# A fused attention and FFN kernel: Mish with fewer VectorE operations, and a new written-out order for the first FFN

## The chip, the cores and the metric

The kernel runs on one core of a Trainium2 chip. The time is the device time of one execution in microseconds. Engines are TensorE (PE), VectorE (DVE), ScalarE (ACT), GpSimd (POOL) and SyncE (SP), which here issues the transfers.

## What is computed

```python
x = attention(q, k, v)            # 2 x 8 heads, 768 x 64; keys 0..7 and the last 96, slope bias
h = x @ w_in                      # 1536 x 512 @ 512 x 2048, float64 weights
sp = where(h > 20, h, log1p(exp(min(h, 20))))
x = (h * tanh(sp)) @ w_out        # Mish, back to 1536 x 512
p = probs / (probs.sum(-1) + 1e-9)
out = sum(p[:, e] * (relu(x @ w1[e]) @ w2[e]) for e in range(4))   # 512 -> 1024 -> 512
```

## The kernel before

The 1536 tokens are worked on in three blocks of 512. For the first block, attention (16 pairs of heads and 128-row tiles) and then the first FFN run by themselves; behind them comes a loop over steps in which the experts of block 0, then the FFN of blocks 1 and 2 go on, with the attention of blocks 1 and 2 woven into the first 31 steps. A last stage does the experts of blocks 1 and 2.

**The first FFN** has 16 steps, one for each 128 columns of `w_in`. A step s consists of these pieces, each with a letter in the string `PLAN`, which `first_block` executes letter by letter and which so fixes the order on every engine:

- narrowing chunk s of the weights from float64: `a` is ScalarE's Abs (L602), each `t` is one of three VectorE operations (L605, L607, L609). The float64 chunk is a 1 MB load into one of four buffers (`big`, `raw`; the list `TURN` says which); a finished chunk is also stored to DRAM (L613, 0.5 MB), and the next load into the buffer is issued when the third `t` is through.
- `H`: the hidden group on TensorE (L783, four f32 matmuls of 512 columns).
- Mish of the 128x512 tile h. With E = exp(h) and n = E(E+2), it is h n/(n+2), where r = 1/(n+2) is made by ScalarE as exp(-ln(n+2)) and then refined by a Newton step: `e` ScalarE Exp (L663), `c` cap (L670), `n` (L677), `l` ScalarE's Ln and Exp (L682, L683), then u (L687), m (L692), v (L698) and the gate g (L702), all on VectorE but `e` and `l`.
- `P`: the project group (L795, four matmuls into four accumulator banks).

`w` letters split the first expert chunks into two fp32r parts (L629 on ScalarE, L632 on VectorE). At the string's end `i` issues the loads of the next attention pairs (SP), `j` splits their queries and keys into parts (L234, L236 on ScalarE, L239, L241 on GpSimd for the first two pairs and on VectorE after that), and `1` to `6` are the parts of one attention round: load ahead, scores s (L260, L261), softmax (L274, L285), normalization and splits of further pairs (L190 to L195, L249, L250), transposes pt (L200, L297, L298), and o (L307, L315). A round's transposes and o belong to the one and two rounds before it, so a round started alone has neither.

**The loop** (`run`) does in step s the hidden group H of twelve fp32r matmuls (L647), one attention round and the project group P of step s - 1 (L748). Step 16 is its first. At steps 23, 31 and 39 (`EXTRA = 7, 15, 23`) a second, extra round is done around the hidden group. The FFN steps in it use the same Mish functions, with `e` in PSUM.

Of the kernel before, what the change touches and what calls it, by code (L numbers as in the profile page):

```python
# [15 lines left out]
P = 128  # L16
# [8 lines left out]
NF1 = 16  # L25
# [18 lines left out]
    "CSEZAEADVVFTXTCEZAAaDVVTtTCaAZtAFtHtttteHcatntlHteaumcvnegcPtlatumtHvngtlPteuamvcHgntltaPeucmtvgHntl"  # L44
    "tauPetmvgcPntltauHtmvgtePcntlatHutmteHvcagntltPeumavgHcntltuPetmcvnHgtlutPmevgcntlPumvgHtttePtcnlHau"
    "mtvtaHgetictnPetlcutHmwvgnwlPweuwcmvgHnwlwuwmPevcgnwlwPumvgjj1P23456"
# [4 lines left out]
    "l": ["n"], "u": ["l"], "m": ["u"], "v": ["m"], "g": ["v"], "P": ["g"],  # L51
# [3 lines left out]
TURN = [0, 1, 2, 3, 0, 1, 2, 3, 0, 1, 2, 3, 0, 1, 0, 1]  # L55
FREE = {2: 4, 3: 8}
EXTRA = 7, 15, 23
# [100 lines left out]
class Pair:  # L158
# [173 lines left out]
class FirstPair(NarrowPair):  # L332
# [206 lines left out]
class Body:  # L539
# [138 lines left out]

    def mish_r(self, s):

        nc, (e, n, r) = self.nc, self.enr[s]
        nc.scalar.activation(r, n, AF.Ln, bias=2.0)  # L682
        nc.scalar.activation(r, r, AF.Exp, scale=-1.0)  # L683

    def mish_u(self, s):
        nc, (e, n, r) = self.nc, self.enr[s]
        nc.vector.scalar_tensor_tensor(e, n, 2.0, r, ALU.add, ALU.mult)  # L687

    def mish_m(self, s):
        nc, (e, n, r) = self.nc, self.enr[s]  # L690
        self.nr[s] = self.temp("nr", s, bufs=1)
        nc.vector.tensor_tensor(self.nr[s], n, r, ALU.mult)  # L692

    def mish_v(self, s):
        nc, (e, n, r) = self.nc, self.enr[s]
        nr = self.nr.pop(s)
        self.enr[s] = e, n, nr if e is r else r
        nc.vector.scalar_tensor_tensor(self.enr[s][2], e, 2.0, nr, ALU.subtract, ALU.mult, reverse0=True)  # L698
# [321 lines left out]
    def first_block(self, ready, now):  # L1020
# [5 lines left out]
        n = dict.fromkeys("SXEDNTCAFHecnlumvgPatw", 0)  # L1026
# [77 lines left out]
        def begin_next(k):  # L1104
            assert n["t"] >= 36
            then.load(4)
# [7 lines left out]
            "u": self.mish_u, "m": self.mish_m, "v": self.mish_v, "g": self.gate_first, "P": project,  # L1114
# [12 lines left out]
        return then, n["P"]  # L1127


    def run(self):  # L1130
# [39 lines left out]
        for s in range(s0, last):  # L1170
# [143 lines left out]
```

## Time and profile before

| | us |
|---|---|
| median of 3 runs (lowest to highest) | 902.6 (899.82 to 902.76) |
| the profiled execution | 900.72 |
| its span | 898.8 |

| engine | busy us | share of the span |
|---|---|---|
| PE, matmuls | 875.3 | 97% |
| PE, weight loads | 669.8 | 75% |
| DVE | 622.9 | 69% |
| ACT | 453.5 | 50% |
| POOL | 380.4 | 42% |

The share is a mean over stages with different limits. Matmuls are pipelined, so an interval in which PE counts as busy may still hold some lost time; it is found by comparing when the same kind of group starts. The four stages are the first attention (up to 37 us), the first FFN (to 154), the loop (to 549) and the last stage. A row of a timeline gives start, duration, engine, line, operation, tiles written <- read, shape and count, and in brackets the engine's idle time before it and what ended it.

### The profile page before, as it was taken

What the parts mean: (1) busy time and instruction counts of PE and PEld (TensorE: products, weight loads), DVE (VectorE), ACT (ScalarE), POOL (GpSimd) and SP (SyncE); (2) the same over time, 40 slices, a digit from 0 to 9 for tenths busy, and PEclk for the clock granted to TensorE, in tenths of its full rate; (3) what the DMA queues carried; (4) which work ended last, traced back from release to release, by engine and by line L of the source; (5) the groups of instructions that cost most, each with busy time, mean ns of one, the idle gap of its engine ahead of it and who ended that gap; (6) DMA issues with size and microseconds to landing.
All of it is one profiled execution on the core that took longest, in us unless ns stands there. A gap on an engine that the chain in (4) does not pass through costs nothing.

```text
span 898.8 us, 11323 instructions
## 1 busy us (share of the span) xinstructions
PE 875.3 (97%) x3848; PEld 669.8 (75%) x3848; DVE 622.9 (69%) x1208; ACT 453.5 (50%) x895; POOL 380.4 (42%) x416
## 2 busy tenths in 40 slices
PE   9899999999999999999999999899999999999997
PEld 5534444788888888888888887688888888888886
DVE  6999988867778686588878887435555455554555
ACT  7653335778777776556554456443333333333330
POOL 4000002487868776544401114455544455555420
PEclk9999999999999999999999999999999999999999
DMA  9487361554344442778655650521111111211002
GB/s 325 186 316 261 131 231 50 188 185 167 141 152 153 174 154 72 275 268 299 247 198 187 234 187 1 164 71 47 48 48 47 47 47 47 59 59 47 1 2 97
DMA packets 39859, 126.16 MB, mean 140 GB/s; under 512 B 4080, under 2 KB 6896, under 8 KB 37744
## 3 DMA queue, kind: packets, MB, share of 16 engines
q1 hardware_dynamic: 39648, 125.32, 39.3%
q8 instruction: 32, 0.52, 0.2%
q14 instruction: 35, 0.29, 0.1%
q10 hardware_dynamic: 144, 0.02, 0.0%
HBM read 97.02 MB, written 28.31 MB: 139 GB/s over the span
## 4 chain that ended last, share of the span: by engine, by line
PE 84%; DVE 7%; ACT 3%; DMA 2%; issue 1%; POOL 1%; SPq 0%; DVEq 0%; ACTq 0%; POOLq 0%
PE acc_l L949 20%; PE h L647 18%; PE acc L748 18%; PE ha L904 9%; PE hx L904 7%; PE acc L795 3%; PE h L783 3%; PE pt L200 2%; PE o L307 2%; ACT p L285 1%; DMA big<-in_wff 1%; DVE r L698 1%; DMA w<-in_wts 1%; DMA qk<-in_qk 1%; PE s L261 1%
## 5 line engine op out<-in xcount | busy, mean ns | idle before, releaser
L808 DVE SCALAR_TENSOR_TENSOR big<-acc_l,prob,big 128x512 f32<-128x512 f32 x120 | 88.7, 746 | 77.8 <-PE acc_l L949 77.7
L632 POOL TENSOR_TENSOR wl<-w,wh 128x512 fp32r<-128x512 f32 x90 | 114.8, 1296 | 65.6 <-ACT wh L629 61.7
L887 POOL TENSOR_TENSOR zl<-wout,zh 128x512 fp32r<-128x512 f32 x32 | 40.9, 1300 | 82.5 <-ACT zh L885 82.5
L887 POOL TENSOR_TENSOR sumsl<-bias,sumsh 128x512 fp32r<-128x512 f32 x32 | 41.0, 1302 | 73.4 <-ACT sumsh L885 73.4
L911 ACT COPY raw<-ha 128x512 f32<-128x512 f32 x33 | 19.3, 586 | 81.7 <-PE ha L904 81.7
L783 PE MATMUL h<-x,w 128*128 128x512 f32 x128 | 57.0, 593 | 0.7 <-ACT x L407 0.7
L195 POOL TENSOR_SCALAR p<-p,st 128x256 f32<-128x256 f32 (+1 forms) x58 | 41.5, 727 | 37.8 <-ACT v L249 33.7
L239 POOL TENSOR_TENSOR qs<-raw,qs 64x256 fp32r<-64x256 f32 x2 | 1.9, 967 | 123.3 <-ACT qs L234 123.2
L748 PE MATMUL acc<-wh,gh 128*128 128x512 f32 x128 | 52.5, 410 | 0.0
L629 ACT CAST wh<-w 128x1024 fp32r<-128x1024 f32 x48 | 50.2, 1047 | 1.8 <-DMA w<-in_wts 1.1
L949 PE MATMUL acc_l<-zh,gh 128*128 128x512 f32 x128 | 50.7, 396 | 0.0
L285 ACT ACTIVATE p<-t,st 128x256 f32<-128x256 f32 (+1 forms) x96 | 46.3, 484 | 8.5 <-DVE st L274 8.2
L647 PE MATMUL h<-y0h,wh 128*128 128x512 f32 x128 | 50.4, 394 | 0.0
L949 PE MATMUL acc_l<-zh,gl 128*128 128x512 f32 x128 | 50.5, 394 | 0.0
L949 PE MATMUL acc_l<-zl,gh 128*128 128x512 f32 x128 | 50.3, 393 | 0.0
L949 PE MATMUL acc_l<-zh,gl_late 128*128 128x512 f32 (+1 forms) x128 | 50.3, 393 | 0.0
L949 PE MATMUL acc_l<-zh,gh_late 128*128 128x512 f32 (+1 forms) x128 | 50.3, 393 | 0.0
L647 PE MATMUL h<-y0l,wh 128*128 128x512 f32 x128 | 50.2, 392 | 0.0
L647 PE MATMUL h<-y0h,wl 128*128 128x512 f32 x128 | 50.2, 392 | 0.0
L748 PE MATMUL acc<-wh,gl 128*128 128x512 f32 x128 | 50.2, 392 | 0.0
L748 PE MATMUL acc<-wl,gh 128*128 128x512 f32 x128 | 50.0, 390 | 0.0
L949 PE MATMUL acc_l<-zl,gh_late 128*128 128x512 f32 (+1 forms) x128 | 49.9, 390 | 0.0
(240 smaller groups left out, 2514.6 us busy)
## 6 DMA issues: line engine op xcount, KB each, us to landing
w<-in_wts SPq DMA_DIRECT2D x32, 512.0 KB, 4.5
raw<-in_qkv SPq DMA_DIRECT2D x32, 512.0 KB, 3.6
big<-in_wff SPq DMA_DIRECT2D x10, 1024.0 KB, 6.8
wfirst<-w SPq DMA_DIRECT2D x16, 512.0 KB, 3.0
w<-wfirst SPq DMA_DIRECT2D x16, 512.0 KB, 4.2
wkeep<-wh SPq DMA_DIRECT2D x16, 512.0 KB, 3.0
wkeep<-wl SPq DMA_DIRECT2D x16, 512.0 KB, 2.9
wh<-wkeep SPq DMA_DIRECT2D x16, 512.0 KB, 3.2
```

The costliest lines, as they stand in the source:

```text
L195: engine.tensor_scalar(self.p[:, j, 0:self.nk * P], self.p[:, j, 0:self.nk * P], st[:, 2 + j:3 + j], 0.0, ALU.mult, ALU.add)
L285: nc.scalar.activation(p[:, j, 0:n], t[:, j, 0:n], AF.Exp, bias=self.least[:, j:j + 1], scale=-1.0, accum_out=self.sum[:, j:j + 1])
L629: (nc.vector.tensor_copy if copy == "vector" else nc.scalar.copy)(hi, w)
L632: getattr(nc, engine or "gpsimd").tensor_tensor(lo[:, c], w[:, c], hi.bitcast(F32)[:, c], ALU.subtract)
L647: nc.tensor.matmul(ps, a[:, c], r[:, kc, :], start=m == 0, stop=m == 3 * KC - 1)
L748: nc.tensor.matmul(acc[:, h], a, r, start=opens and k == 0 and m == 0, stop=closes and k == len(chunks) - 1 and m == 2)
L783: self.nc.tensor.matmul(ps, self.w32[s][:, kc * P:(kc + 1) * P], self.x0[:, kc, :], start=kc == 0, stop=kc == KC - 1)
L795: self.nc.tensor.matmul(acc, w[:, 512 + d * P:512 + (d + 1) * P], g, start=s == 0, stop=s == NF1 - 1)
L808: nc.vector.scalar_tensor_tensor(o, acc, p, o, ALU.mult, ALU.add)
L887: nc.gpsimd.tensor_tensor(lo[:, c], w[:, c], hi.bitcast(F32)[:, c], ALU.subtract)
L904: nc.tensor.matmul(ps, a[:, c], r[:, kc, :], start=opens and n == 0, stop=n == 5, skip_group_check=True)
L949: nc.tensor.matmul(o, a[:, c], r[:, w], start=n == 0, stop=n == 5)
```

## The change

Mish: attention's normalization now multiplies its divisor by 0.5, so x and h are twice as large as before, and Exp has scale 0.5. With n = E + 1 (capped), e = n squared, made by ScalarE's Square, and r = 1/(e + 1), the Newton step gives -r, and the gate is (0.5 - r) times 2h. VectorE does cap, u, v and gate; n and m are gone. This holds for all 48 FFN steps. ScalarE's program keeps the one table load that it had. The number of TensorE's program rows stays at 7076.

Order: `PLAN` is written anew; `TURN` runs 0 to 3 throughout; the last two project groups are merged bank by bank (`Q`, `last`); three rounds of the next attention (letters `1` to `6`, three times) stand at the end of `PLAN` instead of one; only step 31 has an extra round (`EXTRA = 15,`); in step 17 the project group of step 16 is issued directly after that step's scores (`follow`).

```diff
 PLAN = (
-    ...
+    ...
 )
-TURN = [0, 1, 2, 3, 0, 1, 2, 3, 0, 1, 2, 3, 0, 1, 0, 1]
+TURN = [0, 1, 2, 3] * (NF1 // 4)
-EXTRA = 7, 15, 23
+EXTRA = 15,
-        nc.vector.tensor_scalar(r, r, 1e-9, None, ALU.add)
+        nc.vector.tensor_scalar(r, r, 1e-9, 0.5, ALU.add, ALU.mult)
...
     def mish_exp(self, s):
-        nc.scalar.activation(e, self.h[s], AF.Exp)
+        nc.scalar.activation(e, self.h[s], AF.Exp, scale=0.5)
     def mish_cap(self, s):
+        e, n = self.enr[s]
+        self.nc.vector.tensor_scalar(n, e, E20, 1.0, ALU.min, ALU.add)
     def mish_n(self, s):
+        e, n = self.enr[s]
+        self.nc.scalar.activation(e, n, AF.Square)
     def mish_r(self, s):
+        nc.scalar.activation(n, e, AF.Ln, bias=1.0)
+        nc.scalar.activation(n, n, AF.Exp, scale=-1.0)
     def mish_u(self, s):
+        nc.vector.scalar_tensor_tensor(self.nr[s], e, 1.0, n, ALU.add, ALU.mult)
-    def mish_m(self, s):
-        nc.vector.tensor_tensor(self.nr[s], n, r, ALU.mult)
     def mish_v(self, s):
+        nc.vector.scalar_tensor_tensor(self.nr[s], self.nr[s], 2.0, n, ALU.subtract, ALU.mult)
     def mish_g(self, s, out=None):
-        nc.vector.tensor_tensor(e if out is None else out, r, self.h.pop(s), ALU.mult)
+        nc.vector.scalar_tensor_tensor(e if out is None else out, self.nr.pop(s), 0.5, self.h.pop(s), ALU.add, ALU.mult)
...
-    def project_first(self, s):
+    def project_first(self, *steps):
...
         for d, acc, _ in self.acc:
+            for k, s in enumerate(steps):
+                self.nc.tensor.matmul(acc, w[k][:, 512 + d * P:512 + (d + 1) * P], g[k], start=s == 0, stop=s == NF1 - 1)
...
+        def last(k):
+            self.project_first(NF1 - 2, NF1 - 1)
...
         def begin_next(k):
-            assert n["t"] >= 36
+            assert n["t"] == 3 * NF1
             then.load(4)
...
+            follow = bool(s0) and s == NF1 + 1
+            if follow:
+                self.project(done)
+                done += 1
             if att and not extra:
                 att.trans()
...
-            if done <= s - (1 if s0 and att and s < need[0] - 2 else 2):
+            if not follow and done <= s - (1 if s0 and att and s < need[0] - 2 else 2):
                 self.project(done)
```

What this does to the engines' programs is shown at three places. Names carry the step's number (h3, gh0, w12) or the block's tile and pair (s4_0); gates are called gh and gl in turn. L783 and L795 are L770 and L783 after the change, L682 and L683 are L676 and L677, and L671 is the Square.

At the start of the first FFN, on TensorE, before:

```order
L783 MATMUL h0_603<-x0_173,w0_405 128x512 x4
L783 MATMUL h1_618<-x0_173,w1_488 128x512 x4
L783 MATMUL h2_633<-x0_173,w2_565 128x512 x4
L795 MATMUL acc0_0_658<-gh0_655,w0_405 128x512
L795 MATMUL acc0_1_659<-gh0_655,w0_405 128x512
L795 MATMUL acc0_2_660<-gh0_655,w0_405 128x512
L795 MATMUL acc0_3_661<-gh0_655,w0_405 128x512
L783 MATMUL h3_678<-x0_173,w3_586 128x512 x4
```

and after:

```order
L770 MATMUL h0_603<-x0_173,w0_405 128x512 x4
L770 MATMUL h1_614<-x0_173,w1_488 128x512 x4
L770 MATMUL h2_633<-x0_173,w2_565 128x512 x4
L770 MATMUL h3_650<-x0_173,w3_586 128x512 x4
L783 MATMUL acc0_0_669<-gh0_648,w0_405 128x512
L783 MATMUL acc0_1_670<-gh0_648,w0_405 128x512
L783 MATMUL acc0_2_671<-gh0_648,w0_405 128x512
L783 MATMUL acc0_3_672<-gh0_648,w0_405 128x512
```

The fourth hidden group now stands ahead of the first project group.

In the middle of the first FFN, on ScalarE, around step 6, before:

```order
L663 ACTIVATE e6_802<-h6_789 128x512
L682 ACTIVATE r6_803<-n6_804 128x512
L683 ACTIVATE r6_803<-r6_803 128x512
L602 ACTIVATE w11_816<-raw1_123 128x1024
L663 ACTIVATE e7_831<-h7_820 128x512
L602 ACTIVATE w12_843<-big0_124 128x1024
```

and after:

```order
L602 ACTIVATE w11_782<-raw1_123 128x1024
L663 ACTIVATE e6_803<-h6_787 128x512
L602 ACTIVATE w12_807<-big0_124 128x1024
L671 ACTIVATE e6_803<-n6_804 128x512
L676 ACTIVATE n6_804<-e6_803 128x512
L677 ACTIVATE n6_804<-n6_804 128x512
L602 ACTIVATE w13_828<-big1_125 128x1024
```

The narrowings of chunks 11 and 12 have moved ahead of step 6's Square, Ln and Exp.

At the end of the first FFN, TensorE up to the loop's first hidden group, before:

```order
L795 MATMUL acc0_3_661<-gh14_1073,w14_966 128x512
L795 MATMUL acc0_0_658<-gl15_1088,w15_974 128x512
L795 MATMUL acc0_1_659<-gl15_1088,w15_974 128x512
L795 MATMUL acc0_2_660<-gl15_1088,w15_974 128x512
L795 MATMUL acc0_3_661<-gl15_1088,w15_974 128x512
L260 MATMUL s4_0_1118<-kh4_0_1092,qs4_0_1090 128x256
L261 MATMUL s4_0_1118<-kl4_0_1095,qs4_0_1090 128x256
L260 MATMUL s4_0_1118<-kh4_0_1092,qs4_0_1090 128x256
L261 MATMUL s4_0_1118<-kl4_0_1095,qs4_0_1090 128x256
L647 MATMUL h16_1145<-y0h_1108,wh16_1018 128x512
```

TensorE there after the change:

```order
L783 MATMUL acc0_3_672<-gl13_1025,w13_828 128x512
L307 MATMUL o4_0_1166<-pt4_0_1082,v4_0_1045 128x256 x4
L783 MATMUL acc0_0_669<-gh14_1075,w14_853 128x512
L783 MATMUL acc0_0_669<-gl15_1136,w15_871 128x512
L783 MATMUL acc0_1_670<-gh14_1075,w14_853 128x512
L783 MATMUL acc0_1_670<-gl15_1136,w15_871 128x512
L783 MATMUL acc0_2_671<-gh14_1075,w14_853 128x512
L783 MATMUL acc0_2_671<-gl15_1136,w15_871 128x512
L783 MATMUL acc0_3_672<-gh14_1075,w14_853 128x512
L783 MATMUL acc0_3_672<-gl15_1136,w15_871 128x512
L647 MATMUL h16_1192<-y0h_1181,wh16_913 128x512
```

and VectorE from the gate of step 14 to the cap of step 15 after the change:

```order
L690 SCALAR_TENSOR_TENSOR gh14_1075<-nr14_1072,h14_1017 128x512
L298 TENSOR_TENSOR pt4_0_1082<-pt4_0_1077,pt4_0_1082 128x4x128
L190 TENSOR_SCALAR st4_1_1067<-st4_1_1067 128x2
L191 RECIPROCAL st4_1_1067<-st4_1_1067 128x2
L195 TENSOR_SCALAR p4_1_1065<-p4_1_1065,st4_1_1067 128x256 x2
L239 TENSOR_TENSOR qs4_3_1097<-raw1_123,qs4_3_1097 64x256
L241 TENSOR_TENSOR kl4_3_1102<-raw1_123,kh4_3_1099 128x512
L632 TENSOR_TENSOR wl18_1091<-w18_708,wh18_1090 128x512 x2
L667 TENSOR_SCALAR n15_1120<-e15_1119 128x512
```

The last two project groups alternate by bank, scores, transposes and o of the first three rounds are ahead of them, and the VectorE work of these rounds stands between the last gates.

## Rows read from the trace of the kernel before

**Rows 1.** Stretches: length, busy us (instructions) of each engine, clock, DMA share, GB/s.

```profile
37.38:75.17 37.79, 34.84 (x80) 15.04 (x80) 35.43 (x50) 16.12 (x22) 0.00 (x0) 1.00 0.85 312
...
134.63:153.93 19.30, 17.14 (x40) 7.46 (x41) 16.66 (x25) 9.70 (x17) 4.85 (x4) 1.00 0.17 60
```

**Rows 2.** TensorE's timeline in the first FFN, where four matmuls count as x8.

```profile
37.38 10.57 PE L783 MATMUL h<-x,w 128*128 128x512 f32 x24 [0.69 <-ACT x L407]
49.96 3.67 PE L795 MATMUL acc<-gh,w 128*128 128x512 f32 x8 [2.01 <-DVE gh L702]
53.47 3.60 PE L783 MATMUL h<-x,w 128*128 128x512 f32 x8
56.90 3.60 PE L795 MATMUL acc<-gl,w 128*128 128x512 f32 x8
...
75.17 3.70 PE L795 MATMUL acc<-gh,w 128*128 128x512 f32 x8 [0.94 <-DVE gh L702]
...
134.63 3.70 PE L795 MATMUL acc<-gh,w 128*128 128x512 f32 x8 [0.82 <-DVE gh L702]
...
150.79 3.70 PE L795 MATMUL acc<-gl,w 128*128 128x512 f32 x8 [2.16 <-DVE gl L702]
```

**Rows 3.** Instruction groups by form, VectorE then ScalarE, 37 to 150 us.

```profile
L609 DVE SCALAR_TENSOR_TENSOR w<-big,w 128x1024 int32<-128x1024 int32 x10 | 12.2, 1221 | 0.1
...
L692 DVE TENSOR_TENSOR nr<-n,r 128x512 f32<-128x512 f32 x16 | 11.5, 719 | 0.0
...
L677 DVE SCALAR_TENSOR_TENSOR n<-e 128x512 f32<-128x512 f32 x16 | 11.0, 688 | 0.2
...
L605 DVE TENSOR_SCALAR w<-w 128x1024 int32<-128x1024 int32 x15 | 10.3, 689 | 0.8 <-ACT w L602 0.8
...
L670 DVE TENSOR_SCALAR e<-e 128x512 f32<-128x512 f32 x16 | 6.7, 421 | 1.7 <-ACT e L663 1.7
...
L682 ACT ACTIVATE r<-n 128x512 f32<-128x512 f32 x16 | 10.1, 629 | 32.8 <-DVE n L677 24.3 <-DVE gh L702 4.8 <-DVE gl L702 3.6
L663 ACT ACTIVATE e<-h 128x512 f32<-128x512 f32 x16 | 9.3, 589 | 14.7 <-PE h L783 14.7
```

**Rows 4.** TensorE's timeline: first matmul of H16, H18, H20 and H21.

```profile
154.80 0.40 PE L647 MATMUL h<-y0h,wh 128*128 128x512 f32 x1
...
167.73 0.39 PE L647 MATMUL h<-y0h,wh 128*128 128x512 f32 x1
...
182.54 0.39 PE L647 MATMUL h<-y0h,wh 128*128 128x512 f32 x1
...
189.46 0.39 PE L647 MATMUL h<-y0h,wh 128*128 128x512 f32 x1
```

**Rows 5.** Chain that ended last: H30, H32 and H33, and a step of the second FFN.

```profile
258.88 2.77 PE h L647 x12
...
274.87 2.76 PE h L647 x12
...
281.79 2.76 PE h L647 x12
...
390.72 2.72 PE h L647 x12
```

**Rows 6.** Stretches as in rows 1, and a row of ScalarE's timeline.

```profile
66.00:67.00 1.00, 1.00 (x4) 0.48 (x3) 1.00 (x3) 0.00 (x0) 0.00 (x0) 1.00 0.89 266
58.00:71.00 13.00, 13.00 (x31) 5.70 (x30) 11.18 (x17) 5.05 (x7) 0.00 (x0) 1.00 0.98 359
...
43.99 1.17 ACT L602 ACTIVATE w<-big 128x1024 f32<-128x1024 f32 x1 [2.28 <-DMA big<-in_wff]
```

**Rows 7.** Timeline of VectorE, then of GpSimd, at the end of the first FFN.

```profile
147.10 1.22 DVE L692 TENSOR_TENSOR nr<-n,r 128x512 f32<-128x512 f32 x1
148.35 1.67 DVE L698 SCALAR_TENSOR_TENSOR r<-e,nr 128x512 f32<-128x512 f32 x1
...
146.89 0.88 POOL L239 TENSOR_TENSOR qs<-raw,qs 64x256 fp32r<-64x256 f32 x1 [123.24 <-ACT qs L234]
```

More of the change, by code (lines that the diff above doesn't have):

```diff
@@ L43 @@
     "SSYXXESYSEXSEDXNXESNTDCTXSENAZNEXATTSCZEDAXANSFSNEXTTDCNEZAXANTETSCZaADXNAtSFNTEXSCTXEAZSEDAVSVaXTTX"
-    "CSEZAEADVVFTXTCEZAAaDVVTtTCaAZtAFtHtttteHcatntlHteaumcvnegcPtlatumtHvngtlPteuamvcHgntltaPeucmtvgHntl"
-    "tauPetmvgcPntltauHtmvgtePcntlatHutmteHvcagntltPeumavgHcntltuPetmcvnHgtlutPmevgcntlPumvgHtttePtcnlHau"
-    "mtvtaHgetictnPetlcutHmwvgnwlPweuwcmvgHnwlwuwmPevcgnwlwPumvgjj1P23456"
+    "CSEZAEADVVFTXTCEZAAaDVVTtTCaAZtAFtHttttHetactntlHteauvgHcetntltaPuavgcetPntltauHvgctntlPteauvgHctntl"
+    "tPeuavgctnPtltauvHgtttPecattnltHuvgatPtectnltHtauvgHetcattnHlteuvgPcetntltHwuvgctnPtltieuvHgcwnwlPeu"
+    "vgcnljHwjuvgwP12ecnlwHuvg34612Pecnl3uvg5Hw4w6w12Pecnl3uvg54P6Q"
 )
@@ L657, in mish_exp @@
         if self.first and t == 0:
-            e, r = self.temp("e", s), self.temp("r", s, bufs=1)
+            e, n = self.temp("e", s), self.temp("n", s, bufs=1)
         else:
-            e = r = self.bank(f"e{s}")
-        self.enr[s] = e, self.temp("n", s, bufs=1), r
-        nc.scalar.activation(e, self.h[s], AF.Exp)
+            e, n = self.bank(f"e{s}"), self.temp("n", s, bufs=1)
+        self.enr[s] = e, n
+        nc.scalar.activation(e, self.h[s], AF.Exp, scale=0.5)
     def mish_cap(self, s):
-        e, n, r = self.enr[s]
@@ L679, in mish_r @@
+    def mish_n(self, s):
+        e, n = self.enr[s]
+        self.nc.scalar.activation(e, n, AF.Square)
     def mish_r(self, s):
-        nc, (e, n, r) = self.nc, self.enr[s]
-        nc.scalar.activation(r, n, AF.Ln, bias=2.0)
-        nc.scalar.activation(r, r, AF.Exp, scale=-1.0)
+        nc, (e, n) = self.nc, self.enr[s]
+        nc.scalar.activation(n, e, AF.Ln, bias=1.0)
+        nc.scalar.activation(n, n, AF.Exp, scale=-1.0)
     def mish_u(self, s):
-        nc, (e, n, r) = self.nc, self.enr[s]
@@ L687, in mish_u @@
-        nc.vector.scalar_tensor_tensor(e, n, 2.0, r, ALU.add, ALU.mult)
-    def mish_m(self, s):
-        nc, (e, n, r) = self.nc, self.enr[s]
+        nc, (e, n) = self.nc, self.enr[s]
         self.nr[s] = self.temp("nr", s, bufs=1)
-        nc.vector.tensor_tensor(self.nr[s], n, r, ALU.mult)
+        nc.vector.scalar_tensor_tensor(self.nr[s], e, 1.0, n, ALU.add, ALU.mult)
     def mish_v(self, s):
[L695 to L698, printed above, removed]
+        nc, (e, n) = self.nc, self.enr[s]
@@ L788, in gate_first @@
         self.enr.pop(s)
-    def project_first(self, s):
-        w, g = self.w32.pop(s), self.g.pop(s)
-        if s == 0:
-            self.acc = [(d, self.acc_ps.tile([P, 512], F32, tag=f"acc{d}", name=f"acc{s}_{d}"), None) for d in range(4)]
+    def project_first(self, *steps):
+        w, g = [self.w32.pop(s) for s in steps], [self.g.pop(s) for s in steps]
+        if steps[0] == 0:
+            self.acc = [(d, self.acc_ps.tile([P, 512], F32, tag=f"acc{d}", name=f"acc0_{d}"), None) for d in range(4)]
         for d, acc, _ in self.acc:
-            self.nc.tensor.matmul(acc, w[:, 512 + d * P:512 + (d + 1) * P], g, start=s == 0, stop=s == NF1 - 1)
-        if s == NF1 - 1:
+            for k, s in enumerate(steps):
+                self.nc.tensor.matmul(acc, w[k][:, 512 + d * P:512 + (d + 1) * P], g[k], start=s == 0, stop=s == NF1 - 1)
+        if steps[-1] == NF1 - 1:
             self.end_ffn(0)
@@ L1025, in first_block @@
         then = Attention(self, self.pair, 1, NB - 1)
-        n = dict.fromkeys("SXEDNTCAFHecnlumvgPatw", 0)
+        n = dict.fromkeys("SXEDNTCAFHecnluvgPatw", 0)
         narrowing = [self.narrow(c) for c in range(NF1)]
@@ L1079, in project @@
             self.project_first(s)
+        def last(k):
+            assert n["P"] == NF1 - 2 and n["g"] == NF1
+            self.project_first(NF1 - 2, NF1 - 1)
         def begin(c):
@@ L1113, in first_block @@
             "Y": warm, "H": hidden, "e": self.mish_exp, "c": self.mish_cap, "n": self.mish_n, "l": self.mish_r,
-            "u": self.mish_u, "m": self.mish_m, "v": self.mish_v, "g": self.gate_first, "P": project,
+            "u": self.mish_u, "v": self.mish_v, "g": self.gate_first, "P": project, "Q": last,
             "i": begin_next, "j": lambda k: then.split(k + 1),
@@ L1126, in first_block @@
         ready["narrow"], ready["part"] = NF1, NF1 + n["w"] // 3
-        return then, n["P"]
+        return then, NF1
     def run(self):
```

16 lines of the change are left out of this document (3 added, 13 removed).

## The prediction

> **What bounds the kernel now.** I began with the stretches of the span, then TensorE's own timeline in the first FFN, then what VectorE and ScalarE do there, then the loop behind it.
>
> The stretch view [rows 1] shows TensorE at work for 34.84 of 37.79 us at the start of the first FFN, and 17.14 of 19.30 at its end; the granted clock is 1.00, the upper level of 2.4 GHz, in both. So TensorE is the bound nearly everywhere, and no matmul goes away (TensorE has 7076 program rows before and after): a gain can only be TensorE's lost time. VectorE is the second: 35.43 us of the same 37.79.
>
> TensorE's timeline [rows 2] shows where the first FFN loses. It has 32 groups of four 512-column f32 matmuls (16 steps, a hidden group and a project group each), started 3.43 us apart (53.47 to 56.90). Four waits stand between 37.38 and 153.93: 2.01, 0.94, 0.82 and 2.16 us, 5.93 in all, each for a gate (L702), VectorE's last operation in a step's Mish.
>
> Why the gate is late is in the groups of instructions [rows 3]. VectorE's Mish in a step is cap 0.42, n 0.69 and m 0.72, with u, v and gate alike in shape, and narrowing one weight chunk is 0.69 + 1.22 + 1.22: 7.0 us against 6.87 us of TensorE. Recorded durations overlap a little, or this would not fit; but VectorE is nearly full, and any hiccup lands on TensorE. ScalarE stood idle 32.8 us in front of its Ln, mostly for VectorE's n.
>
> Behind the FFN, TensorE's steps [rows 4]: H16 starts at 154.80, H18 at 167.73, H20 at 182.54, H21 at 189.46. A full step is 6.92 us: two groups of twelve matmuls at 2.77 and one attention round at 1.38. From H16 to H20 four steps less one project group and one o (about 0.47) would need 24.4 us; 27.7 passed, so 3.3 were lost, 1.0 of them after H18 (14.81 for two steps of 6.92). This is where the attention rounds start: the first ones have neither transposes nor o ready.
>
> The loop's extra rounds [rows 5]: the two steps around one (H30 at 258.88, H32 at 274.87) take 15.99 us, where 2 x 6.92 + 1.38 would be 15.22: 0.77 lost per extra round.
>
> **The change part by part.**
>
> *Mish.* Per step VectorE loses n and m (0.69 + 0.72) and gains nothing; ScalarE gains a Square of 512 columns, which the trace does not show: between its Exp at 0.59 and its Ln at 0.63 [rows 3], taken at 0.59. ScalarE's program keeps its single table load, so no reload comes with it. VectorE's u, v and gate are now one dependent chain, each taken at 0.72. So VectorE needs at most 0.42 + 2.16 + 3.13 = 5.7 us of 6.87 in a step, ScalarE about 1.17 [rows 6] + 0.59 + 0.59 + 0.63 + 0.63 = 3.6. Both are clear of TensorE. In the second and third FFN the same edit is worth nothing: TensorE's groups follow each other there without a wait, 2.72 us each (390.72 in [rows 5]).
>
> Here the row speaks first: a two-input VectorE operation of 512 columns takes 0.69 us, ScalarE's 0.59 to 0.63 [rows 3], and ScalarE is the idle engine. The Trainium skill ("ScalarE: Activation LUTs", section "Rules for kernel authors") says the opposite of the edit: multiplications belong on VectorE. By it 16 Squares would stay there, 16 x 0.69 = 11.0 us of VectorE, 6.4 of 6.87 in a step; if the waits at 75.17 and 134.63 stayed with them, the sum below would be 1.8 less, 896.3. This trace is fp32, and I go by the row.
>
> *Order of the FFN.* H3 is moved ahead of P0. H0 starts at 37.38 and four hidden groups last until 51.1; the first gate now comes before that (P0 could start at 49.96 before, with two VectorE operations more in the chain). The 2.01 goes. The waits at 75.17 and 134.63 go with VectorE's load. The last two project groups now run bank by bank (Q), so evictions of y0 start before the last matmul, and H16 follows at once.
>
> What is late next: weights. The narrowings now run ahead of the steps, and ScalarE's Abs (L602), which waits for the transfer, stands in front of a step's Square, Ln and Exp. The worst place is w12, ahead of Square 6. Chunk 4 lands at 43.9 [rows 6]; until chunk 12 there are eight loads of 1 MB with eight stores of 0.5 and three expert loads of 0.5, 13.5 MB. At the 359 GB/s of a full stretch [rows 6] they take 37.6 us: 81.5. Then Abs 1.1, Square 0.6, Ln and Exp 1.3, u, v and gate 2.1: gate 6 at 86.6. TensorE gets to P6 after 14 groups, 37.38 + 48.1 = 85.4. A wait of 1.2 takes the place of the old ones (none at 373 GB/s, 14.3 at 266, the slowest microsecond of that stretch).
>
> *Three rounds at the end of the FFN.* Before, one score stood ahead of H16; now three scores, two transposes and one o stand between the last groups, six pieces of about 0.46 (a third of a round's 1.38). That is moved work, not new. It also moves VectorE's biased sums, scalings and splits ahead of the last gate. H15 ends at 37.38 + 28 groups x 3.433 + three pieces 1.4 + the 1.2 = 136.1; s, P12, pt, P13 and o then last until 144.3, and the first use of gate 15 comes a quarter group later, at 145.2. Behind gate 14 VectorE's queue holds nine operations ahead of cap 15 (a transpose's low part, two for the norm, two scalings, two splits, two weight parts); some run before H15 ends, and at up to 0.69 each [rows 3] I put them at 3.7 of delay. Then come cap 0.42, Square 0.6, Ln and Exp 1.3, u, v, gate 2.1, from 139.8 to 144.2. That just fits; I allow 0.4 for it. First FFN: 5.93 - 1.2 - 0.4 = 4.3 gained. Of the queues, SP issues the attention loads behind the sixteenth chunk's store, whose narrowing now stands ahead of u10 in VectorE's order; P10 is due near 121, so they are out by about 115 and not waited for.
>
> *Start of the loop.* With three rounds begun, pt and o of step 16 have inputs that are done, and P16 is moved directly behind the next scores. Of 3.3 lost, the 1.0 after H18 has other causes (ScalarE waiting for a chunk, GpSimd's first scalings) and I leave it: 2.3 gained. Bounds: 0 and 3.3.
>
> *Extra rounds.* Two of three go: 2 x 0.77 = 1.5. Bounds: 0 and 1.5.
>
> Sum: 4.3 + 2.3 + 1.5 = 8.1 us against the profiled execution's 900.72 (span 898.8 and 1.9 around it), so 892.6. The median of the runs, 902.6, lies 1.9 above that execution; a median is what will be measured, so the **forecast is 894.5**. With everything lost gone it would be 5.9 + 3.3 + 1.5 = 10.7, 891.9.
>
> **The rivals.**
>
> *GpSimd takes VectorE's time at the end of the FFN.* While GpSimd ran a two-input subtraction (from 146.89 on), VectorE's m and v took 1.22 and 1.67 instead of 0.69 [rows 7]: 1.5 us, most of the old wait of 2.16. The new order has the same four GpSimd splits earlier (ahead of the first scores, more than a dozen us before P12 needs the gate they delay), but puts three more subtractions (v of each round) beside the last gates. If each costs 0.75, 2.2 us come back at the end, and about 0.9 behind it: gain 5.0, 897.6. The Trainium skill ("GPSIMD Engine Reference", section "Specifications") says that GpSimd shares SBUF interfaces with VectorE and contends with its operations of two SBUF inputs; u and v are such, and the rows agree. Chance 0.16.
>
> *The lost time only moves.* The loop's stalls come from the attention chain itself and reappear a few steps later; only the FFN's 4.3 is kept: 898.3. Against it: from H20 on steps are full. Chance 0.11.
>
> *Weights hold ScalarE (slower).* The Abs in front of each Square makes transfers the pace of the FFN. At 266 GB/s, P6 is 14.3 late: 902.6 + 14.3 - 5.9 - 2.3 - 1.5 = 907.1. It decides below about 276 GB/s, held for 50 us. For it: 266 [rows 6] and the ScalarE waits for big<-in_wff. Against: 359 over 13 us with the same mix. Chance 0.07.
>
> *Nothing.* The waits were not VectorE's load but other handovers, and stay: within 0.3% of before. Chance 0.05; 0.61 is left for the forecast.
>
> **How the numbers follow.** A run of this kernel can be told from no change beyond about 0.3%, 2.7 us. Forecast, first and second rival lie beyond it, though the rivals' edges (and some of the forecast's) reach within: faster 0.81, same 0.12, slower 0.07. The range runs from 890.0, a little beyond the full 10.7 us (each restart after a wait also takes 3.70 instead of 3.60), to 900.5, which takes in both milder rivals and leaves the slower one out.
>
> **What would show it.** Right: no wait for a gate before P0; TensorE's waits until H16 under 2 us, at P6 if anywhere; H16 near 152 (144.3, two project groups of 3.43, the 0.4 and a restart) with six attention pieces already done; H16 to H18 in about 11 us; one long pair of steps instead of three. Wrong: waits at P4 to P6 whose chain leads to big<-in_wff; m-like rows of 1.2 us and more on u and v near the last gate; new waits for p or o around steps 18 to 22.

## The result, and the profile after

The changed kernel takes 892.91 us in the median of four runs (892.46 to 893.69), beside 901.82 (899.82 to 902.76) for the kernel before: ratio 0.9905, 95% interval 0.9885 to 0.9925. The profiled execution has 892.84, with a span of 891.0; spans of single executions are compared from here on, 898.8 before and 891.0 after.

The groups of instructions in the order of their cost, by form, VectorE and then ScalarE (busy us, mean ns, idle time before them):

```profile
L686 DVE SCALAR_TENSOR_TENSOR nr<-nr,n 128x512 f32<-128x512 f32 x48 | 34.3, 714 | 1.6
L682 DVE SCALAR_TENSOR_TENSOR nr<-e,n 128x512 f32<-128x512 f32 x48 | 33.2, 692 | 53.3 <-ACT n L677 53.3
...
L671 ACT ACTIVATE e<-n 128x512 f32<-128x512 f32 x48 | 29.4, 612 | 24.2 <-DVE n L667 24.1
L676 ACT ACTIVATE n<-e 128x512 f32<-128x512 f32 x48 | 29.3, 609 | 1.6
```

Mish is as announced: u (L682) 0.69, v (L686) 0.71, and the Square on ScalarE (L671) 0.61. VectorE is busy 566.5 us, 56.4 less than before; ScalarE 481.8, 28.3 more. What this gave is on TensorE's timeline in the first FFN (H is L770 now, P is L783):

```profile
38.15 14.00 PE L770 MATMUL h<-x,w 128*128 128x512 f32 x32 [0.69 <-ACT x L407]
51.99 3.60 PE L783 MATMUL acc<-gh,w 128*128 128x512 f32 x8
...
69.15 3.60 PE L783 MATMUL acc<-gl,w 128*128 128x512 f32 x8
75.33 5.40 PE L783 MATMUL acc<-gh,w 128*128 128x512 f32 x8 [2.58 <-DVE gh L690]
80.57 3.60 PE L770 MATMUL h<-x,w 128*128 128x512 f32 x8
...
90.95 3.70 PE L783 MATMUL acc<-gh,w 128*128 128x512 f32 x8
...
125.39 3.60 PE L783 MATMUL acc<-gh,w 128*128 128x512 f32 x8
129.29 3.60 PE L770 MATMUL h<-x,w 128*128 128x512 f32 x8
...
150.04 1.12 PE L783 MATMUL acc<-gl,w 128*128 128x512 f32 x2 [0.27 <-DVE gl L690]
...
155.75 0.79 PE L647 MATMUL h<-y0h,wh 128*128 128x512 f32 x1
```

None of the four waits of before [rows 2] is left. In their place stands one of 2.58 us before P4 (75.33), and the group behind it takes 5.40 us where others take 3.60: 1.80 more, at a lower granted clock. The stretch view has the clock there, 0.95 in the mean of 35 us (microsecond by microsecond it is 0.50, the lower level of 1.2 GHz, from 76 to 79 us, and 1.00 again from 80 on), and the transfers (in the stretch of [rows 1] the DMA engines are busy 0.94 of the time, 0.85 before):

```profile
37.38:75.17 37.79, 34.68 (x82) 15.11 (x80) 33.55 (x42) 20.63 (x29) 0.00 (x0) 1.00 0.94 364
...
75.33:110.00 34.67, 34.66 (x77) 15.12 (x78) 31.52 (x39) 18.71 (x26) 0.00 (x0) 0.95 0.62 223
```

ScalarE's timeline tells why gate 4 was late:

```profile
64.28 0.58 ACT L663 ACTIVATE e<-h 128x512 f32<-128x512 f32 x1
70.13 1.13 ACT L602 ACTIVATE w<-big 128x1024 f32<-128x1024 f32 x1 [5.27 <-DMA big<-in_wff]
71.17 0.61 ACT L671 ACTIVATE e<-n 128x512 f32<-128x512 f32 x1
71.81 0.63 ACT L676 ACTIVATE n<-e 128x512 f32<-128x512 f32 x1
72.48 0.63 ACT L677 ACTIVATE n<-n 128x512 f32<-128x512 f32 x1
```

The Abs (L602) of chunk 9 stands ahead of step 4's Square in ScalarE's queue. It waits 5.27 us for its transfer, and Square, Ln and Exp, which need nothing of it, wait with it: VectorE's cap, the Square's input, was done at 67.1.

In the loop, TensorE's timeline has the first matmuls of H18, H19 and H20 at

```profile
167.44 0.39 PE L647 MATMUL h<-y0h,wh 128*128 128x512 f32 x1
...
174.35 0.39 PE L647 MATMUL h<-y0h,wh 128*128 128x512 f32 x1
...
181.26 0.39 PE L647 MATMUL h<-y0h,wh 128*128 128x512 f32 x1
```

and the chain that ended last (start, us, what) has, further on,

```profile
263.90 3.04 PE h L647 x12
...
271.69 2.76 PE h L647 x12
...
354.25 5.48 PE h L647 x24
```

From H18 on a step takes 6.91 us; before, the stretch from H18 to H20 alone took 14.81 [rows 4]. One pair of long steps is left, the one that ends at 271.69. The row of 24 matmuls at 354.25, where the woven attention ends, stood at 360.09 before.

The stretches between such landmarks, in us (the last stage begins at 548.49 before and at 542.32 after):

| stretch | before | after | less |
|---|---|---|---|
| up to H0 (unchanged) | 37.38 | 38.15 | -0.77 |
| H0 to H16 | 117.42 | 117.60 | -0.18 |
| H16 to H20 | 27.74 | 25.51 | 2.23 |
| H20 to the row of 24 | 177.55 | 172.99 | 4.56 |
| FFN of blocks 1 and 2 | 188.40 | 188.07 | 0.33 |
| last stage | 350.31 | 348.68 | 1.63 |

The first FFN looks unchanged, but it holds five attention pieces more, at 0.47 each (125.39 to 129.29 is 3.90 where two groups without a piece stand 3.43 apart): 2.3 us of work moved in, so 2.1 gained. Likewise two rounds of 1.38 left the stretch behind H20, so of its 4.56 us 1.8 are gain; and from H16 to H20 four steps less P's 2.77 would need 24.9, so 0.6 is lost there where 3.3 was lost. The last stage is not touched by the change. Its waits are the same in both; what differs is the granted clock in its first part, 0.97 before and 1.00 after (the first row is of the kernel before):

```profile
545.00:600.00 55.00, 50.81 (x211) 39.98 (x210) 28.82 (x39) 31.14 (x45) 27.95 (x26) 0.97 0.26 84
545.00:600.00 55.00, 50.81 (x217) 40.09 (x217) 28.86 (x38) 29.87 (x43) 27.16 (x26) 1.00 0.30 96
```

### The profile page after: what moved, and what is told of

The parts are those of the page before. It is cut to its first block, busy times and chain, and to the rows that moved or that the text cites. A ratio compares the mean times of both kernels' runs of the same rounds, so it can differ in the third digit from the quotient of the medians.

```text
span 891.0 us, 11253 instructions
## 1 busy us (share of the span) xinstructions
PE 873.6 (98%) x3848; PEld 669.6 (75%) x3848; DVE 566.5 (64%) x1112; ACT 481.8 (54%) x943; POOL 385.9 (43%) x416
## 4 chain that ended last, share of the span: by engine, by line
PE 80%; DVE 9%; ACT 4%; DMA 3%; issue 2%; POOL 0%; SPq 0%; DVEq 0%; ACTq 0%; POOLq 0%
PE acc_l L937 20%; PE h L647 19%; PE acc L735 19%; PE ha L892 9%; PE hx L892 7%; DMA big<-in_wff 2%; PE pt L200 2%; PE o L307 2%; DVE w L607 1%; DVE w L609 1%; ACT p L285 1%; DVE nr L686 1%; DVE nr L682 1%; PE acc L783 1%; DMA raw<-in_wff 1%
## 5 line engine op out<-in xcount | busy, mean ns | idle before, releaser
L632 POOL TENSOR_TENSOR wl<-w,wh 128x512 fp32r<-128x512 f32 x90 | 118.8, 1340 | 60.2 <-ACT wh L629 55.1
L682 DVE SCALAR_TENSOR_TENSOR nr<-e,n 128x512 f32<-128x512 f32 x48 | 33.2, 692 | 53.3 <-ACT n L677 53.3
L663 ACT ACTIVATE e<-h 128x512 f32<-128x512 f32 x48 | 28.0, 584 | 60.1 <-PE h L647 25.4
L770 PE MATMUL h<-x,w 128*128 128x512 f32 x128 | 56.8, 593 | 0.7 <-ACT x L407 0.7
L274 DVE CUSTOM_DVE_ANT_0 t<-s,bias 128x256 f32<-128x256 f32 (+1 forms) x96 | 34.5, 399 | 24.7 <-PE s L261 20.8
```

Of the source, the lines that this page charges most:

```text
L632: getattr(nc, engine or "gpsimd").tensor_tensor(lo[:, c], w[:, c], hi.bitcast(F32)[:, c], ALU.subtract)
L682: nc.vector.scalar_tensor_tensor(self.nr[s], e, 1.0, n, ALU.add, ALU.mult)
L770: self.nc.tensor.matmul(ps, self.w32[s][:, kc * P:(kc + 1) * P], self.x0[:, kc, :], start=kc == 0, stop=kc == KC - 1)
```

## The experiments

**Mish alone, and the order alone.** The first kernel is the one before with the new Mish; its written order (without `m`), `TURN`, `EXTRA = 7, 15, 23` and the order of the loop stay (and `n` has two buffers, one in the changed kernel). The second is the changed kernel with the old Mish and `m` put back into its order. The expectations speak of a fifth operation; in the kernels the old Mish has six operations on VectorE in a step, the new one four, and ScalarE does the Square.

```diff
 # Mish alone, against the changed kernel
-TURN = [0, 1, 2, 3] * (NF1 // 4)
+TURN = [0, 1, 2, 3, 0, 1, 2, 3, 0, 1, 2, 3, 0, 1, 0, 1]
-EXTRA = 15,
+EXTRA = 7, 15, 23
-            follow = bool(s0) and s == NF1 + 1
+            follow = False
 # the order alone, against the changed kernel
-    "l": ["n"], "u": ["l"], "v": ["u"], "g": ["v"], "P": ["g"],
+    "l": ["n"], "u": ["l"], "m": ["u"], "v": ["m"], "g": ["v"], "P": ["g"],
```

> The kernel before with the new Mish alone: its own written-out order (the letter m taken out), its expert order and its three extra rounds stay. Theory (the order does most of it, Mish makes room for it): only part of the 5.9 us of waits inside the first FFN goes, because ScalarE now does one more operation a step in an order that was laid out for VectorE: 899 to 901, 1 to 3 us under the kernel before, and no gain at the start of the loop, where H16 to H20 should still lose about 3 us. Rival 1 (VectorE's fifth operation alone caused the waits): 896.5 to 898. Rival 2 (ScalarE becomes the bound at once): 902 or more.

> The changed kernel with the old five-operation Mish put back, its new order, expert order and single extra round kept. Theory (the new order needs the shorter Mish): VectorE has 0.6 to 0.7 us more a step, in the first FFN and in the dense last rounds, so gates come late there: 897 to 901, 4 to 8 us over the changed kernel. Rival (the order alone carries the gain and Mish is off the path): 892 to 894, the time of the changed kernel.

Mish alone: 894.83 us (893.37 to 895.31), ratio 0.9926 (0.9911 to 0.9942), 6.5 less than before. That is more than the theory's 1 to 3, and a little more than rival 1 had (896.5 to 898), whose mechanism was right: VectorE's additional operations caused nearly all the waits. Its timeline has one left, before P0, and H16 comes 112.48 us after H0 (37.34), where before it took 117.42:

```profile
49.71 3.67 PE L783 MATMUL acc<-gh,w 128*128 128x512 f32 x8 [1.80 <-DVE gh L690]
...
149.82 0.40 PE L647 MATMUL h<-y0h,wh 128*128 128x512 f32 x1
```

Its loop is that of before: 205.24 us from H16 to the row of 24 matmuls, 205.29 before. So a first FFN without waits takes 112.48 - 1.80 = 110.7 with its one attention piece, and every other kernel's first FFN can be measured against that: the kernel before loses 6.7 us there (5.93 in its four waits, the rest in small ones), the changed kernel 117.60 - 2.3 - 110.7 = 4.6.

The order alone: 905.93 us (904.1 to 906.52), ratio 1.0051 (1.0035 to 1.0067): slower than before, by 4.6 (901.35 on that chip), and 13 us slower than the changed kernel; the theory, that the order needs the shorter Mish, held, with a price larger than its 4 to 8. Four of its waits on the way to H16:

```profile
57.18 3.70 PE L796 MATMUL acc<-gl,w 128*128 128x512 f32 x8 [1.78 <-DVE gl L702]
...
77.15 3.70 PE L796 MATMUL acc<-gh,w 128*128 128x512 f32 x8 [2.53 <-DVE gh L702]
...
93.76 3.70 PE L796 MATMUL acc<-gh,w 128*128 128x512 f32 x8 [2.61 <-DVE gh L702]
...
144.90 0.81 PE L200 MATMUL pt<-ident,p 128*128 128x128 f32 x4 [2.44 <-DVE p L195]
```

The two parts are not a sum: -6.5 and +4.6 make -1.9, and together they gave 8.9. On top of the new Mish the order adds about 2: it gains 1.8 before P0, some 2.7 at the start of the loop and 1.8 with the extra rounds, and gives back 4.4 at P4.

**Does the square belong on VectorE?**

```diff
-        self.nc.scalar.activation(e, n, AF.Square)
+        self.nc.vector.tensor_tensor(e, n, n, ALU.mult)
```

> The changed kernel with Mish's square as a product on VectorE, so five operations there again and none on ScalarE, all else as changed. Theory (VectorE is what Mish filled: the old five-operation Mish in the new order took 905.9 us, and the square as a product of two float32 tiles lasts about 0.69 us on VectorE as the others do): about the same, 902 to 906, 9 to 13 us over the changed kernel. Rival (ScalarE, which stands behind the weight transfers, is the limiter and is glad to be rid of the square): 890 to 893.

902.79 us (900.77 to 906.01), ratio 1.0021 (1.0009 to 1.0033); the changed kernel took 892.41 on the same chip. 10.4 us for one operation a step: the theory. Over all 48 steps the product took longer than was reckoned, 0.95 us in the mean (0.75 in the first FFN, 1.06 in the others):

```profile
L671 DVE TENSOR_TENSOR e<-n 128x512 f32<-128x512 f32 x48 | 45.7, 951 | 1.2
```

Beside the changed kernel's profile of the same chip, 7.3 of the time went in the first FFN (124.56 us from H0 to H16, 117.24 there) and 3.9 in the FFN of blocks 1 and 2 (191.95 and 188.08). The second part is not a full VectorE: in eleven steps from 391 to 447 us GpSimd's weight split (L632, two in 2.83 us) runs over the product, which then takes 1.6 us, and these steps follow each other every 5.77 us; later, without GpSimd, the product takes mostly 0.70 and a step 5.44. In the first FFN ScalarE was not relieved of anything that mattered: the wait before P4 is there (3.35 us), and a second of 2.13 stands before the last gate.

```profile
76.29 5.40 PE L783 MATMUL acc<-gh,w 128*128 128x512 f32 x8 [3.35 <-DVE gh L690]
...
154.64 1.57 PE L783 MATMUL acc<-gl,w 128*128 128x512 f32 x2 [2.13 <-DVE gl L690]
```

**Is it the Abs of chunk 9 that costs the 2.58 us?** In the first of two kernels one `a` moves behind step 4's Ln and Exp. In the second the three expert chunks (0.5 MB each; the expectation below takes them as 1 MB) are fetched six steps later, which leaves their bandwidth to the weights.

```diff
 # one letter, the end of the first line of PLAN
-ctntlPteauvgHctntl"
+ctntlPteuvgHctntla"
 # the late fetch
-            if s == 4:
+            if s == 10:
```

> The changed kernel with one letter moved: ScalarE takes the absolute value of weight chunk 9 behind the logarithm and exponential of step 4 and no longer ahead of its Square. Theory (the 2.58 us before P4, and the lower clock behind it, come from ScalarE standing behind a transfer): the wait before P4 goes under 0.5 us and the clock stays at 1.00 behind it, 2.6 to 4.4 us less than the changed kernel, about 888.5 to 890.3. Rival 1 (the next late chunk, 10 or 12, takes over): a wait of 1 to 2 us before P5 or P6, gain 0.5 to 1.5. Rival 2 (the projection's own chunk w4 or H's weights are late too, since the queue is full): the wait stays, no gain.

> The changed kernel with the three expert chunks that are fetched at step 4 fetched at step 10. Theory (DMA bandwidth makes chunk 9 late): 3 chunks of 1 MB at about 350 GB/s are some 9 us of transfer ahead of nothing urgent; if they stand in the queues ahead of or beside chunk 9, the 2.58 us before P4 shrinks and the time falls by 1 to 4 us (889 to 892). Rival (they are issued too late to hold up chunk 9; they compete only with 12 and 13): the wait before P4 stays within 0.5 us of 2.58, and the time moves by under 0.5 us, or rises where the experts' weights now come late.

One letter: 892.38 us (889.63 to 894.33), ratio 0.9901 (0.9882 to 0.9919), no difference to the changed kernel. P4 now waits 0.44 us, and the wait turns up two project groups later, before P6, whose Square stands behind the Abs of chunk 12. This is rival 1, with a slightly longer wait and without its gain of 0.5 to 1.5, and the place where the prediction had put it.

```profile
72.84 3.70 PE L783 MATMUL acc<-gh,w 128*128 128x512 f32 x8 [0.44 <-DVE gh L690]
...
89.01 5.40 PE L783 MATMUL acc<-gh,w 128*128 128x512 f32 x8 [2.17 <-DVE gh L690]
```

The late fetch: 890.79 us (889.34 to 892.15), ratio 0.9882 (0.9864 to 0.99), as the theory had it. No wait before P4, 1.96 before P6 at an unchanged clock, and 1.06 before a late gate:

```profile
71.92 3.60 PE L783 MATMUL acc<-gh,w 128*128 128x512 f32 x8
...
87.78 3.70 PE L783 MATMUL acc<-gh,w 128*128 128x512 f32 x8 [1.96 <-DVE gh L690]
...
147.66 1.13 PE L783 MATMUL acc<-gl,w 128*128 128x512 f32 x2 [1.06 <-DVE gl L690]
```

Both mend P4, so it was the transfer of chunk 9 and its place ahead of the Square. In the changed kernel the wait at P4 had made TensorE late enough for P6 to wait only 0.08.

**All late chunks out of the way.** The Abs of chunks 9, 10 and 12 go behind Ln and Exp, that of chunk 13 behind an Exp; then the same with the late fetch.

```diff
-ctntlPteauvgHctntl"
-"tPeuavgctnPtltauvHgtttPecattnltHuvgatPtectnlt...
+ctntlPteuvgHctntla"
+"tPeuvgctnPtlatauvHgtttPecttnlatHuvgtPteactnlt...
```

> The changed kernel with four letters moved: ScalarE takes the absolute values of chunks 9, 10 and 12 behind the logarithm and exponential of steps 4, 5 and 6, and that of chunk 13 behind the hidden exponential that it stood ahead of. Theory (it is the place in ScalarE's order that makes the late chunks cost time: with chunk 9 alone moved, P4 waited 0.44 us, but P6 then waited 2.17 for chunk 12, at a lower clock): neither P4 nor P6 waits over 0.5 us, H0 to H16 takes 113 to 114 us where the changed kernel takes 117.6, and the time is 887.5 to 890. Rival 1 (the chunks are so late that a product of the weights themselves is next): a matmul of the hidden layer waits on a weight tile, and the time stays at 891 to 893. Rival 2 (the lost time is the clock's and it falls anyway, at the next wait of over 1 us): the waits go, but a stretch of the last round or of the last stage shows the lower clock, and the time is 890.5 to 892.

> The kernel with the four absolute values moved and, besides, the three expert chunks fetched at step 10 and no longer at step 4. Theory (order and bandwidth are two ends of the same wait, so whichever is mended first leaves the other little): within 1 us of the kernel with the four letters moved alone, 887 to 889.5. Rival 1 (they add up, since bandwidth still limits): 1.5 us or more faster than with the letters alone. Rival 2 (the fetch at step 10 makes the experts' weights late, as the 1.06 us before a gate at 147.66 us in the run of the late fetch alone may show): 0.5 to 2 us slower than with the letters alone.

The four letters: 890.29 us (889.37 to 890.9), ratio 0.9885 (0.9867 to 0.9903). With the late fetch besides: 890.82 (888.93 to 895.22), ratio 0.9895 (0.9874 to 0.9917), the same within 1 us, as the theory had it, though both medians lie above its 887 to 889.5. In the profile of the four letters no wait over 0.4 us is left before P4 or P6, and H16 stands 113.01 us behind H0 (37.62): less 2.3 of moved work that is 110.7, nothing lost.

```profile
72.13 3.60 PE L783 MATMUL acc<-gh,w 128*128 128x512 f32 x8
...
86.17 3.70 PE L783 MATMUL acc<-gh,w 128*128 128x512 f32 x8
...
150.63 0.79 PE L647 MATMUL h<-y0h,wh 128*128 128x512 f32 x1
```

But the span, 887.6, is only 3.4 under 891.0, since the last stage takes 1.7 more at a clock of 0.97 in its first part, as it did before the change. To set the two side by side on one chip, both ran again:

> The changed kernel itself, beside the kernel with the four absolute values moved on the same chip. Theory: its first FFN shows the wait of 2 to 4 us before P4 again, 892 to 893.5 us. Rival (that wait was one execution's): no wait before P4, and no difference to the kernel with the letters moved.

> The changed kernel with the four absolute values moved, again, beside the changed kernel on the same chip. Theory (the wait before P4 is 2.58 us, and 1.8 us of lower clock behind it come only in some executions): 2.5 to 4.4 us under the changed kernel, no wait over 0.5 us in its first FFN. Rival (a fall of the clock later takes what was won): under 1.5 us less.

The changed kernel again: 892.41 (892.19 to 894.61), ratio 0.9913 (0.9899 to 0.9926), with 2.87 us before P4 and a group of 5.40 behind it. The four letters again: 891.0 (890.27 to 892.39), ratio 0.9888 (0.9874 to 0.9903). So 1.4 us less here (2.3 by the two ratios, whose intervals just overlap). Across the earlier runs it is 2.6, but these are from different chips, on which the kernel before took 901.82 and 900.51; taken from that, the gains are 8.9 and 10.2, and 1.3 apart. The version is a little faster than the changed kernel, by less than the 4.4 of its stretch, and nearer to the rival's under 1.5 than to the theory's 2.5. Two things took the rest in the second profile. One is the clock in the first part of the last stage (0.94), where the stage took 2.1 us more than in the changed kernel's profile of the same chip:

```profile
545.00:600.00 55.00, 50.81 (x205) 39.89 (x204) 26.69 (x34) 27.44 (x40) 24.00 (x24) 0.94 0.30 96
```

The other is a wait of 1.16 us for the last gate, which the first profile of this version lacks. It can be followed back to the Abs of the last chunk, 15, on ScalarE's timeline, at 98.01 in this execution and at 95.75 in the earlier one of the same order (TensorE's wait, then the two rows of ScalarE):

```profile
147.18 1.13 PE L783 MATMUL acc<-gl,w 128*128 128x512 f32 x2 [1.16 <-DVE gl L690]
```

```profile
98.01 1.17 ACT L602 ACTIVATE w<-raw 128x1024 f32<-128x1024 f32 x1 [3.04 <-DMA raw<-in_wff]
```

```profile
95.75 1.18 ACT L602 ACTIVATE w<-raw 128x1024 f32<-128x1024 f32 x1 [1.82 <-DMA raw<-in_wff]
```

The last gate starts at 146.43 and 144.18: 48.42 and 48.43 us behind that Abs. In the changed kernel it is 100.85 and 149.29, 48.44, and in four more profiles with this end of the first FFN, where that Abs waits for its transfer too (the late fetch, both, three extra rounds, the changed kernel again) 48.39 to 48.45. In between VectorE's idle time ends with ScalarE each time, never with TensorE. So from the landing of chunk 15 on, VectorE and ScalarE run one chain to the last gate, and its 48.4 us are as long as TensorE's own way there (the changed kernel waits 0.27 for it); with the waits gone, the last landing sets the end of the first FFN.

**The two other parts of the order.** One kernel has a single round at the end of the first FFN and the extra rounds of before in the loop; the other keeps the three rounds and has the extra rounds of before. (In both, the work done is the same, at other places.)

```diff
 # one round
-"vgcnljHwjuvgwP12ecnlwHuvg34612Pecnl3uvg5Hw4w6w12Pecnl3uvg54P6Q"
+"vgcnljHwjuvgwPecnlwHuvgPecnluvgHwwwPecnluvgPQ123456"
-EXTRA = 15,
+EXTRA = 7, 15, 23
-            follow = bool(s0) and s == NF1 + 1
+            follow = False
 # three extra rounds
-EXTRA = 15,
+EXTRA = 7, 15, 23
```

> The changed kernel with one round of the next attention at the end of the first FFN and not three, so with the three extra rounds of the kernel before in the expert loop. Theory (the start of the loop and the extra rounds give about 2.7 and 1.8 us): the first FFN's own waits stay as in the changed kernel (2.6 us before P4), H16 comes about 2.5 us earlier, the steps from H16 to H20 lose 3 us again, and the time is 896 to 898. Rival (the two rounds cost as much inside the first FFN, at its slower matmuls, as they save in the loop): 892 to 894.

> The changed kernel with its three rounds at the end of the first FFN, but with extra rounds of attention at experts 7, 15 and 23 of the loop, as before, and not at 15 alone. (The rounds done in advance then leave the loop earlier without work.) Theory (a longer step where an extra round stands costs 0.6 to 0.9 us each): 893.8 to 895. Rival (an extra round in the loop costs nothing of itself, the time went with the moved work): 892.5 to 893.3.

One round: 898.67 us (897.12 to 899.88), ratio 0.9977 (0.9966 to 0.9989), 5.8 over the changed kernel, or 7.1 when each is taken from the kernel before on its own chip (900.51 here, 901.82 there). Its loop is that of before again, 205.3 us from H16 (154.21) to the row of 24 (359.55); the changed kernel takes 198.5. Of the 6.8 between them, 2.3 are the moved work, 4.5 are gain: 2.7 + 1.8, as read from the trace. What it loses more at P4 (a wait of 3.42, then a group of 6.39: 1.8 more than in the changed kernel) is most of the rest.

Three extra rounds: 895.22 us (893.79 to 896.53), ratio 0.994 (0.9925 to 0.9955), 2.3 over the changed kernel, or 3.6 taken as above. Its loop takes 200.73 us from H16 to the row of 24, 2.2 more than the changed kernel's: two extra rounds more cost 1.1 us each, beyond the 0.6 to 0.9 that was expected. What else the 3.6 holds is open.

Not tried by themselves were the place of P16 in step 17, the last two project groups bank by bank, and `TURN`.

## Why the prediction was right, and which of its steps failed

The forecast was 894.5 with a range to 890.0 and 900.5; 892.91 is 1.6 below it, with the forecast's own mechanism in kind: a shorter Mish and an order that leaves TensorE fewer waits. Half of the 1.6 is the median it starts from, 902.6, which a fourth run made 901.82.

- **Mish**: right. u, v and gate came at 0.69 to 0.71, the Square at 0.61 where 0.59 was taken; all the old waits for a gate but P0's went with the shorter Mish alone, which by itself gave 6.5 us. P0's went with H3 moved ahead of it.
- **"The worst place is w12"**: this step failed. The wait is real, and of the kind described, but it came three chunks earlier, at chunk 9 and P4. The step's own sum shows it when it is made there: five loads, five stores and three expert loads (9 MB at the 359 GB/s of [rows 6], 25.1 us) behind the 43.9 of chunk 4 give a landing at 69.0, measured 70.1; gate 4 at 74.1, P4 due at 71.7, and so a wait of 2.4, measured 2.58. The sum was made for one place and has to be made for each. It also counts a load of 1024 KB as 1.0 MB where the rate counts it as 1.049: put right, chunk 9 lands at 70.2 and gate 4 comes at 75.3 (P4 started at 75.33), a wait of 2.8 with the H0 of this execution, and at the step's own place the 1.2 becomes 3.0. P6's own wait was 1.96 and 2.17 once P4's was out of the way, against the 1.2 of the step.
- **The clock**: the sum had no term for it. The group behind the wait took 5.40 for 3.60 us, so a wait of 2.58 cost 4.4. It was the largest term missing from the sum.
- **First FFN, 4.3**: this term was mis-sized by the two above; 2.1 were measured. The 0.4 for gate 15 held (0.27).
- **Start of the loop, 2.3**: 2.7 measured. The 1.0 behind H18, which the step put down to other causes and left standing, went as well (steps of 6.91 from H18 on). It belongs to the start of the attention: from H18 to H20 it is 14.81 us again in the run with one round, 13.83 in that with three rounds and the old extra rounds.
- **Extra rounds, 1.5**: 1.8 in the trace, 2.2 in the loop of the run that puts them back.
- Of the signs named, "no wait before P0", "H16 to H18 in about 11 us" (11.69) and "one long pair" came true; "H16 near 152" did not (155.75): 0.8 of it is the later H0, the rest P4, which lost 4.4 where 1.2 had been put. "Waits under 2 us, at P6 if anywhere" did not either, and one of the signs of being wrong came: a wait at P4 whose chain leads to big<-in_wff. It took back half of the first FFN's gain and not the whole.
- The terms make 6.6 against 8.1. That the median fell by 8.9 all the same has the last stage behind it in the profiled execution (1.63, the clock), which no term foresaw: so far the agreement is luck. The clock there differs between executions of one order (0.97 and 0.94 in the two profiles of the four letters); whether the change has a part in it is open, since both profiles of the changed kernel had 1.00 and the only one of the kernel before had 0.97.
- **GpSimd takes VectorE's time**: the slowing came as described, ahead of gate 12, which P12 needs at 140.97 only, where VectorE had just stood idle for 2.02 us. VectorE's and GpSimd's timelines:

```profile
123.94 0.69 DVE L682 SCALAR_TENSOR_TENSOR nr<-e,n 128x512 f32<-128x512 f32 x1 [2.02 <-ACT n L677]
124.67 1.10 DVE L686 SCALAR_TENSOR_TENSOR nr<-nr,n 128x512 f32<-128x512 f32 x1
```

```profile
124.34 0.88 POOL L239 TENSOR_TENSOR qs<-raw,qs 64x256 fp32r<-64x256 f32 x1 [99.92 <-ACT qs L234]
125.30 1.62 POOL L241 TENSOR_TENSOR kl<-raw,kh 128x512 fp32r<-128x512 f32 x1
```

  v takes 1.10 beside the two subtractions for 0.69 to 0.71 elsewhere, less than the 1.22 and 1.67 of [rows 7]. The rule of the Trainium skill ("GPSIMD Engine Reference", "Specifications") on shared SBUF interfaces agrees with these rows; of the 0.4 us and what other operations lost beside these splits, no more than the 0.27 before the last gate reached TensorE. The rival's three further subtractions came too (L250, at 135.16, 142.54 and 150.47). Beside the two that stand ahead of the last gate, VectorE's splits took 1.10 and 0.89 us for 0.69 and 0.42: 0.9 lost on VectorE, where the rival had put 2.2 on TensorE.
- **Weights hold ScalarE**: its mechanism is what spoiled the gain, but at the 364 GB/s of the stretch above it cost 4.4 us and not 14.3.
- **The lost time only moves; nothing**: neither. The loop from H16 to the row of 24 took 198.50 us for 205.29, and only 2.3 of that is work done earlier; and the ratio's interval, up to 0.9925, lies clear of 1.
- **The rule against the edit**: the Trainium skill ("ScalarE: Activation LUTs", "Rules for kernel authors") puts multiplications on VectorE, with its speed per element in bf16 as the reason, which by the prediction's reckoning gave 896.3. The run with the product there took 902.8. For a float32 tile of 128x512, Square in 0.61 us and the product in 0.75 or more, the trace does not agree, and beside a nearly full VectorE and GpSimd's splits the cost was larger than the reckoning had.

## What to carry to other kernels

An operation that waits for a transfer, placed ahead of ready work on an in-order engine, lends its lateness to everything behind it; reckon the landing of every such load against the step it stands in front of, not only the one that looks worst, and put it behind that step's chain. Taking two operations a step from the nearly full engine, and giving one to an idle one, was worth 6.5 us by itself, and 13 under an order that left less slack; an edit and an order made for it should be tried apart, since their parts need not add up. Where the last of a set of transfers starts a chain as long as the bound engine's remaining way, reordering that brings this landing no earlier gains nothing more.

## What the runs showed of the hardware

After a wait, TensorE's granted clock sometimes falls, and the group behind then takes 1.8 us more (5.40 for 3.60). It is no matter of the wait's length alone: 2.17 us in one kernel's profile and 2.58 in another were followed by a fall; 2.53 and 2.61 in the order-alone kernel, and 3.52 in that with three extra rounds, were not. The same happens behind the waits early in the last stage, which are alike before and after: behind 1.59 and 0.86 us at 571 the clock of 570 to 575 was 0.71 before, and behind 1.61 and 0.85 at 565 it stayed at 1.00 after. The clock from 545 to 600 us was 1.00 in some profiles, 0.97 in most others and 0.94 in one. The spread of one kernel's executions goes with the granted clock: of 17 runs of the kernel before on one chip, the lowest four (898.46 to 898.66) had a mean granted clock of 0.998 or 0.999, the highest four (901.84 to 902.5) one of 0.995 or 0.996. Whether a fall early makes one later less likely stays open: of five profiles with a long group in the first FFN, three had 1.00 in the last stage's first part; of eight without, two.

Beside GpSimd's subtractions operations of VectorE took longer: v 1.10 us for 0.69, a cap 0.95 for 0.42, the product 1.6 for 0.7.
